# Fast-stage term loads moved to SyncE and shared between chunks, with a replanned instruction order

## The chip, the cores and the metric

The kernel runs as one program on one core of a Trainium2 chip. The metric is the device time of one execution in microseconds (us). The engines are TensorE (PE, matmuls; its weight loads are shown as PEld), VectorE (DVE), ScalarE (ACT), GpSimd (POOL) and SyncE (SP). Each engine takes its own instructions strictly in the order in which the program lists them; DMA transfers are issued from an engine's list too, and then run beside everything else.

## The reference

Two parts follow each other. The first is attention with a feature map, for 8 batches, 8 heads, 576 positions and 64 columns; the second takes its output as 4608 tokens of 512 numbers through a layer of 2048 hidden units with the Mish function.

```python
def phi(x):
    proj = np.einsum('bhsd,df->bhsf', x, w_phi)
    proj = proj - np.max(np.abs(proj), axis=-1, keepdims=True)
    return np.concatenate([np.exp(proj), np.exp(-proj)], axis=-1)
q_p, k_p = (phi(q), phi(k))
kv = np.einsum('bhsf,bhsd->bhfd', k_p, v)
z = np.sum(k_p, axis=2)
num = np.einsum('bhsf,bhfd->bhsd', q_p, kv)
den = np.einsum('bhsf,bhf->bhs', q_p, z)[..., None] + 1e-06
x = num / den                       # seen as [4608, 512]
...
h = x @ w_in                        # [4608, 2048]
sp = np.where(h > 20.0, h, np.log1p(np.exp(np.minimum(h, 20.0))))
return ((h * np.tanh(sp)) @ w_out)  # [4608, 512]
```

## The kernel before

**Tiling.** The tokens are cut into 18 chunks `c` of 256. A chunk needs two attention units, `q{c}_0` and `q{c}_1` (two pairs of heads each), and the sums over keys that they read, which come from 36 key units `k{n}`. For a chunk the hidden layer has 16 tiles `f` of 128 units: `ff_in` (L508) makes one tile with 12 matmuls of 128x256 on PE ("h" in the profile). Numbers are split into a high and a low part, so each product takes three matmuls.

**Output product, plain and fast.** Chunks 0 to 4 multiply by `w_out` directly (`ff_out`, L542, "o" in the profile). From chunk `FAST` = 5 on, two hidden tiles 2m and 2m+1 make a pair of tiles `m` (0 to 7), and `out_fast` (L668) multiplies a pair with 21 matmuls of 128x256 by a scheme with seven products instead of eight ("ox", "oy", "oz", "ow"). Its second operands are sums and differences of blocks of `w_out`. They are computed once (`w_sum`, `combine`; planned from `PREP` with a step of `PSTEP`), sent to DRAM as `terms[m]`, five per pair, and loaded back into SBUF when they are needed: `load_term(c, m, i)` (L661) moves term `i`, 256 KB. The fifth term of every pair stays in SBUF after chunk 5. The other four go into a ring of eight slots, so the terms of pair m can be loaded once the fast product of pair m-2 has been made, and they are loaded again in every chunk. The last two pairs of the last chunk use four tiles of their own ("late").

**A unit's path.** For a query unit: `project` (PE, L327, "pp_q"), maximum and subtraction (DVE, L331 and L339, "m_q" and "e_q"), a block transpose of each of its two halves (DVE, L351), then each half goes to DRAM (`q_send`, SP, L355, "there_e<-e_q") and comes back with four DMAs that finish the transpose (`q_fetch`, SP, L360, "e_q<-there_e"). ACT takes the two exponentials of each half (L428, L429), PE makes the sums over keys ("kvps") and the numerators ("num", both L347), DVE adds and copies the key sums (L411, L414) and divides (L466 to L468). The result goes through DRAM in the same way ("there_x<-via", then "x<-there_x") to become the operand xTh, xTl of `ff_in`. The next unit is projected right after the numerators, when DVE has given a PSUM bank back. `mish_fast` (ACT, L584), `mix` (DVE, L592 to L594), `mix_cast` (ACT, L599) and `mix_rest` (DVE, L603) make the operands of `out_fast`. The exponential and Mish need different tables in ACT; ACT_TABLE_LOAD changes them.

**What sets the order.** No engine chooses anything at run time. The class `Plan` holds a task for each of these steps, with an engine, a key (roughly its due time in tiles of `ff_in`), an assumed duration, its inputs, and the buffers ("rings") that it takes and gives back. `Plan.order()` plays the program through with those assumed durations. An engine that is free takes the first ready task by key, and the sequence so found is the order that is written into the engines' lists. Some tables of numbers (`FIRST_KEYS`, `WKEYS` and so on) are such keys. On the chip a task waits for its real inputs, and everything behind it on that engine waits too. In the kernel before, `order()` gives transfers of POOL and transfers of SP each a bandwidth of their own. Term loads are issued by POOL, and all other transfers by SP.

Of the kernel before, what the change touches and what calls it, by code (L numbers as in the profile page):

```python
# [31 lines left out]
FAST = 5  # L32
NLATE = 2
PAIRED = 0
PSTEP = 2.0
# [3 lines left out]
PREP = 54.0  # L39
# [9 lines left out]
FIRST_KEYS = {0: -16.15, 1: -12.2, 2: -13.99, 3: -10.24, 4: -8.03, 5: 7.54, 6: 8.15, 7: 8.48, 8: 11.95, 9: 27.01, 10: 29.1}  # L49
FIRST_QUERIES = {0: -11.57, 1: -9.11, 2: -2.36, 3: -2.32, 4: 13.79, 5: 9.72}  # L50
NFIRST = 6
E0 = -0.153
E1 = 0.109
GX = 0.616
ET = 0.242
WKEYS = [-9.37, -8.76, -5.05, -1.08, 3.01, 4.23, 4.64, 9.45, 6.86, 10.03, 12.05, 14.27, 15.1, 15.51, 17.23, 20.83,
         22.94, 21.2, 23.28, 26.21, 25.97, 28.3, 28.45, 32.87, 35.29, 34.63, 36.82, 37.72, 39.36, 40.32, 39.03, 41.85]
LAG, TAIL, TAILLAG = 4, 10, 2
TWOH = 99
NEAR = 1.4  # L60
LANDS = 2.297
BEHIND = 1.286
TEXP = 1.065
TLEAD = 2.999
SPLITC = 12
QFIRST = 99
URGENT = 2.075
UCENTRE = -0.038
BURST = ("sum", "num", "project")
PATIENCE = 1.514  # L70


class Plan:
# [11 lines left out]
    def order(self):  # L85
# [6 lines left out]
        now, table, bus, last = 0.0, None, [2.5, 2.5], dict(kind=None)  # L92
# [11 lines left out]
        def ready(task):  # L104
            if any(dep not in done for dep in task["after"]):
                return False
            for dep in task["deps"]:
                if done.get(dep, 1e9) > now:
                    return False
            if any(done.get(dep, 1e9) > now + NEAR for dep in task["near"]):  # L110
                return False
            for ring, _ in task["take"]:
                held_now = sum(released.get(token, 1e9) > now for token in slots.setdefault(ring, []))
                if held_now + sum(r == ring for r, _ in task["take"]) > self.rings.get(ring, 1):
                    return False
            return True

        while any(waiting.values()):
            moved = False
            for engine, queue in waiting.items():  # L120
# [45 lines left out]
            if not moved:  # L166
                times = [t for t in list(free.values()) + list(done.values()) if t > now + 1e-9]
# [7 lines left out]
def attention_then_mish(ctx, tc, qT, kT, va, w_phi, w_in, w_out, out):  # L175
# [10 lines left out]
    plan = Plan(dict(att=4, h=2, o=2, raw=NRAW, e=NE, v=NV, kv=NKV, half=NHALF, xT=NXT, g=NG, u=NU, w=NW, part=NPART, mix=NMIX, fast=2))  # L186
# [461 lines left out]

    def home_of(c, m, i):
        if c == NCH - 1 and m >= NFT // 2 - NLATE and i < 4:  # L650
            tile_of, k = divmod(4 * (m - NFT // 2 + NLATE) + i, 2)
# [5 lines left out]
        else:  # L657
            r = (4 * ((c - FAST) * NFT // 2 + m) + i) % (NFT // 2)
        return half_of(r, 1 - r % 2)

    def load_term(c, m, i):  # L661
        nc.gpsimd.dma_start(home_of(c, m, i).bitcast(F32), terms[m][:, i])  # L662

    def out_fast(c, m):
        if m == 0:
# [15 lines left out]
        for k, half, (ah, al), (bh, bl) in products:  # L681
            for n, (a, b) in enumerate(((ah, bh), (ah, bl), (al, bh))):
                nc.tensor.matmul(ps[k][:, half], a, b, start=(m == n == half == 0), stop=(m == NFT // 2 - 1 and n == 2),  # L683
# [190 lines left out]
    loaded = []  # L874

    def plan_fast(n, c, m):
# [10 lines left out]
        uses = []  # L887
        for i in range(5):
            q = 4 * ((c - FAST) * NFT // 2 + m) + i if i < 4 else f"{m} kept"
            if i == 4 and c > FAST:  # L890
                continue
            again = i < 4 and q >= NFT // 2
            r = q % (NFT // 2) if i < 4 else NFT // 2 + m
            deps = [] if again else [plain_out(FAST - 1, r)] + [f"wsum {r // 2} {r % 2}"]
            take, after = [(f"hs{r}", f"hs:{q}")], [loaded[q - NFT // 2]] if again else []
            if c == NCH - 1 and m >= NFT // 2 - NLATE and i < 4:
                nth = 4 * (m - NFT // 2 + NLATE) + i
                q = f"late {nth}"
                take, after = [] if nth % 2 else [("e", f"late:{nth // 2}")], [f"term {c} {m} {i - 1}"] if nth % 2 else []
# [47 lines left out]
    for n in range(total):  # L947
# [3 lines left out]
            take=[] if f % 2 else [("h", f"h:{c}_{f // 2}")], give=[f"xT:q{c}_{g}" for g in range(2)] if f == NFT - 1 else [])  # L951
# [72 lines left out]
```

## Time and profile before

| | |
|---|---|
| median of 3 runs | 1112.04 us (1109.36 to 1113.77) |
| the profiled execution, its own time | 1114.26 us |
| its span, first to last instruction | 1112.5 us |
| mean granted TensorE clock | 0.989 |
| DVE, ACT, POOL busy in the span | 729.4 us, 678.1 us, 227.2 us |
| term loads (POOL) | 424 of 256 KB |
| all DMA | 241.96 MB, 217 GB/s on average |

A row of a group view names the source line, the engine, the operation, and its output and inputs by the program's names ("h<-xTh,win"), with shape and count; then busy time, mean nanoseconds of one, and the idle time of the engine just before such instructions, with what ended it. A row of the timeline begins with its start in us from the span's start and its length; an idle time before it and what ended it stand in square brackets. "SPq" and "POOLq" rows are the issuing of DMAs.

### The profile page before, as it was taken

The numbers are of one execution on the slowest core, as the hardware profiler recorded it, in microseconds if no ns is written. First come the engines' busy times: TensorE is split into PE (matmuls) and PEld (weight loads), VectorE is DVE, ScalarE is ACT, GpSimd is POOL, SyncE is SP. The second block draws the span as 40 slices with busy tenths as digits, with TensorE's granted clock in tenths as the row PEclk, the third lists the DMA queues.
The fourth block names the chain that finished last, engine by engine and source line by source line (L and its number), as shares of the span: only waits on it lengthen the run. The fifth ranks groups of instructions, "written<-read, shape, count | busy, mean of one in ns | idle before, by whom it ended". The sixth has DMA issues, their size and how long they took to land.

```text
span 1112.5 us, 29851 instructions
## 1 busy us (share of the span) xinstructions
PE 1053.4 (95%) x12208; PEld 1001.7 (90%) x12208; DVE 729.4 (66%) x1668; ACT 678.1 (61%) x1019; POOL 227.2 (20%) x430
## 2 busy tenths in 40 slices
PE   7899999999999999999999999999999998989996
PEld 6888989999988989989889899999999988989996
DVE  6999995687855657666565557666767665656442
ACT  5688895566656555557666676776666645344431
POOL 0000000000011222223223232333232322332441
PEclk9999999999999999999999999999999998999998
DMA  9588643365674676757676778778677757777673
GB/s 353 189 267 291 229 134 101 120 208 179 208 228 146 203 228 214 242 180 246 208 235 212 232 235 255 240 232 264 209 256 233 230 181 241 220 229 228 233 231 130
DMA packets 138953, 241.96 MB, mean 217 GB/s; under 512 B 17984, under 2 KB 74432, under 8 KB 138816
## 3 DMA queue, kind: packets, MB, share of 16 engines
q1 hardware_dynamic: 104896, 128.87, 36.3%
q0 software_dynamic: 33920, 111.18, 31.2%
q8 instruction: 96, 1.57, 0.6%
q14 instruction: 41, 0.34, 0.1%
HBM read 196.46 MB, written 43.52 MB: 216 GB/s over the span
## 4 chain that ended last, share of the span: by engine, by line
PE 56%; DMA 17%; ACT 11%; DVE 9%; issue 3%; SPq 2%; POOL 0%; ACTq 0%; DVEq 0%
PE h L518 20%; PE o L553 9%; DMA e_q<-there_e 5%; PE num L347 5%; PE kvps L347 5%; DMA there_e<-e_q 4%; PE ox L683 4%; DMA x<-there_x 3%; PE oy L683 3%; PE ow L683 3%; PE pp_q L327 2%; PE pp_k L327 2%; SPq L360 2%; PE oz L683 2%; DMA raw_q<-qT 2%
## 5 line engine op out<-in xcount | busy, mean ns | idle before, releaser
L518 PE MATMUL h<-xTh,win 128*128 128x256 f32 x2304 | 439.9, 283 | 3.5 <-ACT u L584 1.9
L662 POOL DMA_DIRECT2D wout<-terms x416 | 222.2, 538 | 865.3 <-PE ow L683 504.9
L518 PEld LDWEIGHTS h<-xTh,win 128*128 128x128 f32 x2304 | 366.0, 189 | 10.2 <-ACT u L584 2.9
L518 PE MATMUL h<-xTl,win 128*128 128x256 f32 x1152 | 324.2, 281 | 0.3 <-DVE xTl L502 0.3
L518 PEld LDWEIGHTS h<-xTl,win 128*128 128x128 f32 x1152 | 218.0, 189 | 2.6 <-DVE xTl L502 0.5
L603 DVE TENSOR_TENSOR sl<-s,sh 128x640 fp32r<-128x640 f32 x104 | 85.6, 823 | 146.5 <-ACT sh L599 111.3
L599 ACT CAST sh<-s 128x640 fp32r<-128x640 f32 x104 | 74.8, 720 | 123.4 <-DVE s L594 107.5
L584 ACT ACTIVATE u<-h 128x512 f32<-128x512 f32 x104 | 62.2, 598 | 91.6 <-PE h L518 90.9
L553 PE MATMUL o<-wout,gh 128*128 128x512 f32 x320 | 101.8, 399 | 0.0
L347 PE MATMUL num<-kv,e_q 128*64 128x66 f32 x2304 | 79.3, 225 | 18.5 <-issue 8.6
L592 DVE TENSOR_TENSOR s<-u 128x256 f32<-128x256 f32 x104 | 42.7, 411 | 81.1 <-ACT u L584 80.9
L347 PEld LDWEIGHTS num<-kv,e_q 128*64 128x64 f32 x2304 | 73.3, 139 | 23.7 <-issue 9.7
L683 PE MATMUL ox<-wout,gh 128*128 128x256 f32 x408 | 82.3, 294 | 8.4 <-DMA wout<-terms 8.3
L347 PEld LDWEIGHTS kvps<-v,e_k 128*64 128x64 f32 x2560 | 78.2, 137 | 10.6 <-issue 3.1
L347 PE MATMUL kvps<-v,e_k 128*64 128x66 f32 x2560 | 83.9, 223 | 3.6 <-ACT e_k L383 1.9
L683 PE MATMUL oy<-wout,sh 128*128 128x256 f32 x416 | 79.6, 284 | 0.0
L683 PE MATMUL ow<-wout,sh 128*128 128x256 f32 x408 | 77.2, 281 | 0.0
L683 PEld LDWEIGHTS ox<-wout,gh 128*128 128x128 f32 x408 | 63.6, 192 | 12.3 <-DMA wout<-terms 6.8
L428 ACT ACT_TABLE_LOAD x41 | 52.6, 1283 | 36.1 <-DMA e_q<-there_e 35.7
L584 ACT ACT_TABLE_LOAD x53 | 68.0, 1283 | 0.9
L553 PEld LDWEIGHTS o<-wout,gh 128*128 128x128 f32 x320 | 55.7, 188 | 10.2
L683 PEld LDWEIGHTS oy<-wout,sh 128*128 128x128 f32 x416 | 64.8, 191 | 0.0
(107 smaller groups left out, 1897.0 us busy)
## 6 DMA issues: line engine op xcount, KB each, us to landing
wout<-terms POOLq DMA_DIRECT2D x416, 256.0 KB, 4.5
there_e<-e_q SPq DMA_DIRECT2D x60, 256.0 KB, 4.0
e_q<-there_e SPq DMA_DIRECT2D x240, 64.0 KB, 4.2
v<-va SPq DMA_DIRECT2D x32, 330.0 KB, 5.0
raw_k<-kT SPq DMA_DIRECT2D x36, 256.0 KB, 4.0
out<-osb SPq DMA_DIRECT2D x36, 256.0 KB, 3.3
raw_q<-qT SPq DMA_DIRECT2D x33, 256.0 KB, 4.3
words_in<-w_in SPq DMA_DIRECT2D x16, 512.0 KB, 6.1
```

Source lines behind the costliest of these rows:

```text
L327: nc.tensor.matmul(ps[j][:, n], raw[rows, n * P:(n + 1) * P], w_phi2[rows], start=True, stop=True)
L347: nc.tensor.matmul(ps[rows], lhsT[h], rhs[h], start=start, stop=stop, skip_group_check=True)
L360: nc.sync.dma_start(dst[32 * b:32 * b + 32].rearrange("i (a m) -> i a m", a=4), src[:, b * P:(b + 1) * P].rearrange("(a i) m -> i a m", a=4))
L428: nc.scalar.activation(e[:, 1, :], e[:, 0, :], AF.Exp)
L518: nc.tensor.matmul(ps, w[:, wcol], x[:, cc % 2, :], start=(n == 0), stop=(n == 11))
L553: nc.tensor.matmul(ps.rearrange("p (k n) -> p k n", k=2), g[:, cols], w, start=(i == first and k == 0), stop=(i == end and k == 2))
L584: nc.scalar.activation(u, h_live.pop((c, fp)).rearrange("p f s -> p (f s)"), AF.Mish)
L592: nc.vector.tensor_tensor(s[:, :CH], u[:, :CH], u[:, CH:], op=ALU.add)
L599: nc.scalar.copy(mix_high[c, fp], mixed[c, fp])
L603: nc.vector.tensor_sub(mix_low[c, fp], mixed.pop((c, fp)), mix_high[c, fp].bitcast(F32))
L662: nc.gpsimd.dma_start(home_of(c, m, i).bitcast(F32), terms[m][:, i])
L683: nc.tensor.matmul(ps[k][:, half], a, b, start=(m == n == half == 0), stop=(m == NFT // 2 - 1 and n == 2), skip_group_check=True)
```

## The change

**Reversed order.** In chunks 6, 8, ... 16 the pairs of tiles are taken from m = 7 down to m = 0, both in `ff_in` and in `out_fast`. `place_of(c, m)` is the place of a pair in its chunk. A chunk therefore begins with the two pairs with which the chunk before it ended, and their eight ring slots still hold the right terms: loads for places 0 and 1 are dropped in chunks 6 to 17. This leaves 424 - 96 = 328 term loads. `start` and `stop` of the accumulation follow the place.

**SyncE.** `load_term` is issued with `nc.sync`, and its task belongs to SP with an assumed 0.42 us. In the plan each such load takes one of `NFLIGHT` = 4 places of a ring "flight", which it gives back when the plan thinks that it has landed. This limits the order only; on the chip nothing waits for it.

**Plan.** For PE tasks after 190 us of planned time, inputs and buffers count as ready up to `-SLACK` = 0.137 us ahead of the planned moment (the constant is negative). All transfers share one assumed bandwidth. Many keys and constants get new values.

```diff
-PSTEP = 2.0
+PSTEP = 1.508
+NFLIGHT = 4
+SLACK = -0.137
-PREP = 54.0
+PREP = 58.757
-FIRST_QUERIES = {0: -11.57, 1: -9.11, 2: -2.36, 3: -2.32, 4: 13.79, 5: 9.72}
+FIRST_QUERIES = {0: -10.8, 1: -8.56, 2: 1.41, 3: -2.12, 4: 12.8, 5: 11.39}
-LANDS = 2.297
+LANDS = 2.451
-TLEAD = 2.999
+TLEAD = 3.609
...
         def ready(task):
+            limit = now - SLACK * (task["engine"] == "PE" and now > 190)
             for dep in task["deps"]:
-                if done.get(dep, 1e9) > now:
+                if done.get(dep, 1e9) > limit:
                     return False
...
                 if found["size"]:
-                    n = engine == "POOL"
-                    bus[n] = max(bus[n], now + took + 0.6) + found["size"] / (250e3 if n else 330e3)
-                    late = max(bus[n] - now - took, LANDS) + BEHIND
+                    bus = max(bus, now + 1.0) + found["size"] / 350e3
+                    late = max(bus - now - took, LANDS) + BEHIND
...
+    def place_of(c, m):
+        return NFT // 2 - 1 - m if c >= FAST and (c - FAST) % 2 else m
...
-            r = (4 * ((c - FAST) * NFT // 2 + m) + i) % (NFT // 2)
+            r = 4 * (m % 2) + i
         return half_of(r, 1 - r % 2)

     def load_term(c, m, i):
-        nc.gpsimd.dma_start(home_of(c, m, i).bitcast(F32), terms[m][:, i])
+        nc.sync.dma_start(home_of(c, m, i).bitcast(F32), terms[m][:, i])
...
-                nc.tensor.matmul(ps[k][:, half], a, b, start=(m == n == half == 0), stop=(m == NFT // 2 - 1 and n == 2),
+                nc.tensor.matmul(ps[k][:, half], a, b, start=(first and n == half == 0), stop=(end and n == 2),
...
-    tiles += [(c, f) for c in range(3, NCH) for f in range(NFT)]
+    tiles += [(c, 2 * place_of(c, f // 2) + f % 2) for c in range(3, NCH) for f in range(NFT)]
...
+            if kind == "ring" and c > FAST and place < 2:
+                ends.append(loaded[m % 2, i][1])
+                continue
...
-            add(f"term {key} {i}", "POOL", n + 0.5 + LAGF - TLEAD + 0.1 * i, 1.2, lambda i=i: load_term(c, m, i),
-                deps=deps + [f"send {m} {min(i // 2, 2)} {p}" for p in range(2)], take=take, size=262144,
-                after=after)
+            add(f"term {key} {i}", "SP", n + 0.5 + LAGF - TLEAD + 0.1 * i, 0.42, lambda i=i: load_term(c, m, i),
+                deps=deps + [f"send {m} {min(i // 2, 2)} {p}" for p in range(2)], size=262144, after=after,
+                take=([] if kind == "late" and nth % 2 else [(slot, token)]) + [("flight", f"flight:{key} {i}")],
+                give=[f"flight:{key} {i}"])
```

Since the plan sets the order, the change moves instructions on every engine. Three places show what matters below. The lines of the changed kernel have numbers that are 2 to 7 higher: L355, L360 and L351 become L357, L362 and L353; the term load L662 becomes L668.

The first place is SP's list around unit q9_0 in the fast stage. "there_e_9_0" is the DRAM copy of one of its halves, "x_1" belongs to the unit before it. Before, the list reads:

```order
L355 DMA there_x_1_7207<-via_1_7182 128x512
L355 DMA there_e_9_0_7252<-e_q_0_7211 128x512
L360 DMA x_1_7163<-there_x_1_7207 32x4x128 x4
L360 DMA e_q_0_7211<-there_e_9_0_7252 32x4x128 x4
L355 DMA there_e_9_0_7334<-e_q_0_7213 128x512
L360 DMA e_q_0_7213<-there_e_9_0_7334 32x4x128 x4
```

The change has there:

```order
L357 DMA there_x_1_7178<-via_1_7153 128x512
L668 DMA wout_0_826<-terms_3930 128x512
L668 DMA wout_0_882<-terms_3930 128x512
L668 DMA wout_0_1059<-terms_3930 128x512
L668 DMA wout_0_1145<-terms_3930 128x512
L357 DMA there_e_9_0_7222<-e_q_0_7182 128x512
L362 DMA x_1_7134<-there_x_1_7178 32x4x128 x4
L357 DMA there_e_9_0_7270<-e_q_0_7184 128x512
L362 DMA e_q_0_7182<-there_e_9_0_7222 32x4x128 x4
L668 DMA wout_0_1395<-terms_4151 128x512
L362 DMA e_q_0_7184<-there_e_9_0_7270 32x4x128 x4
```

Four term loads stand ahead of the unit's first send and one between its two fetches; the second half is now sent before the first half is fetched, and no longer after it. Before, the second send stands behind the first fetch in 12 of the 24 units q6_0 to q17_1; in the change it stands ahead of the first fetch in all 24.

The second place is DVE's list at the same unit: the two transposes of its halves (STREAM_TRANSPOSE), and between them work for pair 5 and for a key unit ("m_k", "e_k"). Before:

```order
L351 STREAM_TRANSPOSE e_q_0_7211<-e_q_0_7211 128x512
L608 TENSOR_TENSOR gl_5_7246<-u_5_7098,gh_5_7100 128x256
L603 TENSOR_TENSOR sl_5_7254<-s_5_7228,sh_5_7244 128x640
L331 TENSOR_REDUCE m_k_7282<-pp_k_7234 128x4
L331 TENSOR_REDUCE m_k_7285<-pp_k_7235 128x4
L339 TENSOR_TENSOR e_k_7287<-pp_k_7234,m_k_7282 128x512
L339 TENSOR_TENSOR e_k_7302<-pp_k_7235,m_k_7285 128x512
L351 STREAM_TRANSPOSE e_q_0_7213<-e_q_0_7213 128x512
```

The change:

```order
L353 STREAM_TRANSPOSE e_q_0_7182<-e_q_0_7182 128x512
L610 TENSOR_TENSOR gl_5_7220<-u_5_7062,gh_5_7064 128x256
L605 TENSOR_TENSOR sl_5_7236<-s_5_7200,sh_5_7218 128x640
L353 STREAM_TRANSPOSE e_q_0_7184<-e_q_0_7184 128x512
L333 TENSOR_REDUCE m_k_7264<-pp_k_7206 128x4
```

The key unit's four instructions have moved behind the second transpose.

The third place is the end of PE's list, in the last chunk. Rows "ox" are the beginnings of fast products and rows "ow" their ends; the number behind "gh_" or "sh_" is the pair. Before, the product of pair 4 follows that of pair 3 directly, as that one follows pair 2 and all later ones follow each other:

```order
L683 MATMUL ow_14926<-wout_0_1419,sh_3_14960 128x256 x2
L683 MATMUL ow_14926<-wout_0_1419,sl_3_14976 128x256
L683 MATMUL ox_14923<-wout_0_1144,gh_4_14955 128x256 x2
L683 MATMUL ox_14923<-wout_0_1144,gl_4_15022 128x256
L683 MATMUL ox_14923<-wout_0_983,gh_4_14955 128x256 x2
```

In the change, the rows ahead of pair 4 are matmuls of `ff_in`:

```order
L520 MATMUL h_14_14995<-xTh_1_14505,win_3_2155 128x256
L520 MATMUL h_14_14995<-xTh_1_14505,win_3_2281 128x256
L520 MATMUL h_14_14995<-xTl_1_14529,win_3_2281 128x256
L520 MATMUL h_14_14995<-xTh_1_14505,win_3_2281 128x256
L690 MATMUL ox_14803<-wout_0_1145,gh_4_14856 128x256 x2
```

There, one tile of h (12 matmuls) stands between pairs 2 and 3, two tiles between pairs 3 and 4, and none behind pair 4. In the first fast chunk the change puts two tiles of h between the products of pairs 4 and 5, where before none stood. Between the projection of a unit q{c}_0 and its numerators, PE's list for most of the chunks 7 to 16 had 7 tiles of h and 4 fast products before, and has 8 and 5 in the change; for q{c}_1 it had 9 and 4 (or 3), and has 8 and 3.

On ACT the exponentials of a unit's two halves were in most units parted by a Mish; in the change they stand side by side, and the list has 130 ACT_TABLE_LOAD where it had 158.

More of the change, by code (lines that the diff above doesn't have):

```diff
@@ L91, in order @@
         done, slots, released, freed = {}, {}, {}, {}
-        now, table, bus, last = 0.0, None, [2.5, 2.5], dict(kind=None)
+        now, table, bus, last = 0.0, None, 2.5, dict(kind=None)
         issued = []
@@ L112, in ready @@
             for ring, _ in task["take"]:
-                held_now = sum(released.get(token, 1e9) > now for token in slots.setdefault(ring, []))
+                held_now = sum(released.get(token, 1e9) > limit for token in slots.setdefault(ring, []))
                 if held_now + sum(r == ring for r, _ in task["take"]) > self.rings.get(ring, 1):
@@ L185, in attention_then_mish @@
     banks = dict(att=ps_att, h=ps_h, o=ps_o)
[L186 removed]
+    plan = Plan(dict(att=4, h=2, o=2, raw=NRAW, e=NE, v=NV, kv=NKV, half=NHALF, xT=NXT, g=NG, u=NU, w=NW, part=NPART, mix=NMIX, fast=2, flight=NFLIGHT))
     nc.scalar.preload_act_table_set("natural_log_exp_and_others")
@@ L886, in plan_fast @@
             give=[f"s:{key}"])
-        uses = []
+        uses, place = [], place_of(c, m)
+        late, ends = place - NFT // 2 + NLATE, [f"g:{key}", f"mix:{key}", f"sh:{key}", f"sl:{key}"]
         for i in range(5):
-            q = 4 * ((c - FAST) * NFT // 2 + m) + i if i < 4 else f"{m} kept"
-            if i == 4 and c > FAST:
+            nth, kind = 4 * late + i, "kept" if i == 4 else "late" if c == NCH - 1 and late >= 0 else "ring"
+            if kind == "kept" and c > FAST:
                 continue
[L892 to L899, printed above, removed]
-            add(f"term {key} {i}", "POOL", n + 0.5 + LAGF - TLEAD + 0.1 * i, 1.2, lambda i=i: load_term(c, m, i),
-                deps=deps + [f"send {m} {min(i // 2, 2)} {p}" for p in range(2)], take=take, size=262144,
-                after=after)
-            if i < 4:
-                loaded.append(f"term {key} {i}")
-            uses.append((f"term {key} {i}", f"hs:{q}"))
@@ new lines, in plan_fast @@
+            if kind == "ring" and c > FAST and place < 2:
+                ends.append(loaded[m % 2, i][1])
+                continue
+            r = 4 * (m % 2) + i if i < 4 else NFT // 2 + m
+            slot, token, after = f"hs{r}", f"hs:{key} {i}", []
+            deps = [plain_out(FAST - 1, r), f"wsum {r // 2} {r % 2}"]
+            if kind == "ring":
+                if (m % 2, i) in loaded:
+                    deps, after = [], [loaded[m % 2, i][0]]
+                loaded[m % 2, i] = f"term {key} {i}", token
+                if c == NCH - 1 or place < NFT // 2 - 2:
+                    ends.append(token)
+            elif kind == "late":
+                slot, token, deps = "e", f"late:{nth // 2}", []
+                after = [f"term {key} {i - 1}"] if nth % 2 else []
@@ L908, in plan_fast @@
-        if c == FAST and m == 0:
+        take = [("o", f"ox:{c}"), ("o", f"oz:{c}"), ("fast", f"oy:{c}"), ("fast", f"ow:{c}")] if place == 0 else []
+        if c == FAST and place == 0:
             take += [("att", "reserved 0"), ("att", "reserved 1")]
-        add(f"out {key}", "PE", when, 2.48, lambda: out_fast(c, m), deps=[f"low {key}", f"mixl {key}"] + [d for d, _ in uses], after=[before_out],
-            take=take, give=[f"g:{key}", f"mix:{key}", f"sh:{key}", f"sl:{key}"] + [t for _, t in uses if t[-4:] != "kept"])
+        add(f"out {key}", "PE", when, 2.48, lambda: out_fast(c, m), deps=[f"low {key}", f"mixl {key}"] + uses, after=[before_out],
+            take=take, give=ends)
```

47 lines of the change are left out of this document (24 added, 23 removed).

## The prediction

> **What bounds the kernel now.** First I read the busy shares on the page, then the busy time by stage.
>
> ```profile
> PE 1053.4 (95%) x12208; PEld 1001.7 (90%) x12208; DVE 729.4 (66%) x1668; ACT 678.1 (61%) x1019; POOL 227.2 (20%) x430
> 0.00:190.00 190.00, 175.27 (x2216) 157.19 (x2218) 163.09 (x366) 147.56 (x234) 0.70 (x6) 1.00 0.66 227
> 190.00:400.00 210.00, 207.54 (x2369) 191.28 (x2365) 143.76 (x312) 126.78 (x204) 17.29 (x32) 1.00 0.58 182
> 400.00:1076.00 676.00, 643.09 (x7417) 626.15 (x7417) 410.90 (x962) 396.67 (x570) 200.68 (x376) 0.99 0.73 229
> 1076.00:1112.50 36.50, 27.48 (x217) 27.07 (x215) 11.69 (x29) 7.14 (x13) 8.54 (x16) 0.91 0.46 155
> ```
>
> A stage row holds its length, then the busy time of PE, PEld, DVE, ACT and POOL, the granted clock, the DMA share and GB/s. PE is the bound, and the change takes no matmul away. What it can win is PE's idle time and slow clock: 14.7 us idle up to 190 us, 2.5 us up to 400, 32.9 us up to 1076 and 9.0 us in the last 36.5 us. The groups of PE's instructions from 400 us on say before what it idles:
>
> ```profile
> L518 PE MATMUL h<-xTh,win 128*128 128x256 f32 x1544 | 293.6, 283 | 3.5 <-ACT u L584 1.9 <-ACT xTh L496 1.6
> L683 PE MATMUL ox<-wout,gh 128*128 128x256 f32 x392 | 79.3, 294 | 8.4 <-DMA wout<-terms 8.3
> L347 PE MATMUL num<-kv,e_q 128*64 128x66 f32 x1408 | 49.2, 227 | 15.1 <-issue 7.4 <-ACT e_q L429 3.4 <-DVE kv L411 3.2
> L327 PE MATMUL pp_q<-w_phi,raw_q 64*128 64x128 f32 x336 | 28.5, 291 | 9.4 <-DVE r L466 3.6 <-DMA raw_q<-qT 3.0 <-DVE x L468 2.8
> ```
>
> The numerators and the projection behind them idle 15.1 + 9.4 = 24.5 us, and the fast products wait 8.4 us for terms. To see why the numerators are late I followed one unit, q9_0, in the timelines of SP, DVE, ACT and PE.
>
> ```profile
> 513.21 1.28 PE L327 MATMUL pp_q<-w_phi,raw_q 64*128 64x128 f32 x16
> 518.79 0.33 SPq L355 DMA_DIRECT2D there_e<-e_q  x1
> 519.22 1.93 SPq L360 DMA_DIRECT2D x<-there_x  x4
> ...
> 519.74 1.29 DVE L331 TENSOR_REDUCE m_k<-pp_k 128x4 f32<-128x512 f32 x2
> 522.14 0.70 DVE L351 STREAM_TRANSPOSE e_q<-e_q 128x512 f32<-128x512 f32 x1
> 523.03 1.73 SPq L360 DMA_DIRECT2D e_q<-there_e  x4
> 524.86 0.37 SPq L355 DMA_DIRECT2D there_e<-e_q  x1
> 531.15 1.76 SPq L360 DMA_DIRECT2D e_q<-there_e  x4
> ...
> 535.82 2.56 PE L347 MATMUL kvps<-v,e_k 128*64 128x66 f32 x80
> 536.29 1.28 ACT L428 ACT_TABLE_LOAD   x1 [0.20 <-DMA e_q<-there_e]
> 538.78 0.71 ACT L599 CAST sh<-s 128x640 fp32r<-128x640 f32 x1
> 540.61 0.42 DVE L414 COPY kv<-kvps 128x264 f32<-128x264 f32 x1
> 540.79 0.42 PE L347 MATMUL num<-kv,e_q 128*64 128x66 f32 x7 [2.41 <-issue]
> ```
>
> Projection ends at 514.5. The first half is sent at 518.8, the second only at 524.9: its transpose stood behind the key unit on DVE, and its send behind the first fetch, which sat in SP's list until 523.0. So the second fetch is issued at 531.15 and landed at 536.3, when ACT's wait ends. Then come table, exponentials, the cast, DVE's L603 and the key sums that stand behind it: 4.5 us from landing to numerators (536.3 to 540.8). PE had nothing to do from 538.4 on. "issue" hides that chain: DVE's copy ends as PE starts.
>
> **The change part by part.**
>
> *Both halves sent before the first fetch.* In the new order the second transpose follows at once on L603, so it could start near 519.7 instead of 522.1. The four term loads ahead of the first send cost SP time that was POOL's:
>
> ```profile
> q1 hardware_dynamic: 104896, 128.87, 36.3%
> q0 software_dynamic: 33920, 111.18, 31.2%
> 517.61 2.13 POOL L662 DMA_DIRECT2D wout<-terms  x4 [10.28 <-PE ow L683]
> ```
>
> POOL needed 2.13 us for four; an SP issue of a send or fetch above takes 0.33 to 0.48 us, so I take 0.43 us for an SP term load, the trace having none (ends 0.33 and 0.53), or 1.7 us for four. Starting at 517.6, they end at 519.3, the first send moves from 518.8 to 519.3, the x fetch ends at 521.3, and the second send goes at 521.4, 3.5 us earlier than before. At the same distances (6.3 us from send to fetch, 5.1 to landing) the second half lands at 532.8.
>
> PE meanwhile has more to do ahead of these numerators: one more tile of h and one more fast product.
>
> ```profile
> 223.38 1.42 PE h L518 x12
> 1086.59 0.40 PE L683 MATMUL ox<-wout,gh 128*128 128x256 f32 x2
> 1089.07 0.40 PE L683 MATMUL ox<-wout,gh 128*128 128x256 f32 x2
> 1089.64 2.14 POOL L662 DMA_DIRECT2D wout<-terms  x4 [4.63 <-PE ow L683]
> 1095.58 0.79 PE L683 MATMUL ox<-wout,gh 128*128 128x256 f32 x2 [3.83 <-DMA wout<-terms]
> ```
>
> A tile takes 1.42 us, a fast product 1089.07 - 1086.59 = 2.48 us, together 3.9 us. The key sums would end near 542.3, while landing plus 4.5 us is 537.3. So a wait of 2.4 us turns into 5.0 us to spare. Units q{c}_1 lose about as much: they have 8 tiles and 3 products instead of 9 and 4. But beside them the change loads no terms for two places. What that is worth shows in the stretch 200:300, where no terms are loaded (first row), against 400:1112 (the other two):
>
> ```profile
> e_q<-there_e SPq DMA_DIRECT2D x32, 64.0 KB, 2.0
> wout<-terms POOLq DMA_DIRECT2D x384, 256.0 KB, 4.6
> e_q<-there_e SPq DMA_DIRECT2D x176, 64.0 KB, 4.8
> ```
>
> A fetch lands in 2.0 us there and in 4.8 us beside terms. A unit without terms beside it gets back up to 2.8 us on a fetch and about as much on a send, more than the 3.9 us. A later unit of before, q11_1, has both sends together, with the terms still there:
>
> ```profile
> 666.29 1.16 PE L327 MATMUL pp_q<-w_phi,raw_q 64*128 64x128 f32 x16
> 671.94 0.91 SPq L355 DMA_DIRECT2D there_e<-e_q  x2
> 677.26 5.64 SPq L360 DMA_DIRECT2D e_q<-there_e  x8
> ```
>
> Its last fetch is issued 15.5 us after its projection (667.45 to 682.9) against 18.4 us for q9_0 (514.5 to 532.9), and its numerators start without a wait. Projections that wait for DVE's L466 and L468 are the same lateness one step on. Bounds: between 0 and -24.5 us. I take three quarters, **-18.5 us**, as the 3.0 us for raw_q and the tight units need not go.
>
> *Terms and the end.* The last three rows above show pair 4 of the last chunk. Pair 2's product ends as pair 3's begins, at 1089.07; then pair 4's terms are issued, and they have landed at 1095.58, 6.5 us later, with only one product of 2.48 us between. In the change two tiles of h follow pair 3, so between the end of pair 2 and pair 4 stand 3 x 1.42 + 2.48 = 6.7 us, no wait. For pair 5 it is 2 x 1.42 + 2.48 = 5.3 us, 1.2 us short. In chunk 5 two tiles come between pairs 4 and 5, 2.8 us against the 2.59 us that PE idled there (row below). Of 8.4 us I keep 1.4: **-7 us** (bounds 0 and -8.4). Dropping 96 loads, 25 of 242 MB, is counted at nothing beyond this; PE's matmuls hide it, and without that cover it would show in these same waits.
>
> *Clock.* There are five stretches at half clock; the wait ahead of the first, then the first and the last:
>
> ```profile
> 406.50 0.77 PE L683 MATMUL ox<-wout,gh 128*128 128x256 f32 x2 [2.59 <-DMA wout<-terms]
> 406.10:409.50 3.40, 3.00 (x14) 3.04 (x15) 1.76 (x3) 2.67 (x4) 0.44 (x1) 0.50 1.05 300
> 1095.60:1099.00 3.40, 3.40 (x16) 3.40 (x17) 0.00 (x0) 0.00 (x0) 0.00 (x0) 0.50 0.57 214
> ```
>
> The others are of 3.4, 6.8 and 3.4 us, 20.4 us in all, each behind a wait of 2 to 4 us. At half clock they cost at most half of that, 10.2 us. If three quarters of the waits go, **-7 us** (bounds 0 and -10.2).
>
> The Trainium skill, "TensorE: Matmul & The Clock Gate", section "Part 1: The HAM clock gate (the "warmup" mystery)", gives an idle window of about 3.4 us as what throttles. By that rule only the wait of 3.83 us would count and the clock term would be about -1.7 us, the sum 1089 us. The trace disagrees: the half clock of the first stretch came with a wait of 2.59 us.
>
> *Costs.* 328 issues of 0.43 us on SP are 141 us in a list that is mostly waiting; what counts is who stands behind them. The x fetch, the second half's send and the loads of raw_q do. The 1.6 us that h waits for xTh (in the first group row) show that x can be late, so I add **+2 us** (0 to 20, were that wait to come in each of 12 chunks). The 0.137 us by which PE may be planned early is a wait of at most that in a burst: 24 units make 3 us at the most; taken as nothing, since the lead of 5 us covers it. The start has new keys, but the same work on the same engines, with DVE 163 of 190 us busy: **0** (within 5 us either way, a third of the 14.7 us idle there).
>
> Sum: -18.5 - 7 - 7 + 2 = -30.5 us. From the profiled execution's own 1114.3 us (span 1112.5) this gives 1083.8, **1084 us**. That execution lies 2.2 us above the median of 1112.0, inside the spread of the three runs (1109 to 1114), so I leave that in.
>
> **The rivals.**
>
> *Slower: SP becomes the queue that PE waits for.* Term loads wait in SP's list for a fast product, and every send and fetch behind them waits too; their bytes go ahead of the fetches in one queue. Four loads are 1.05 MB; by the q0 row 111.18 MB took 31.2% of 1112.5 us, 320 GB/s, so 3.3 us. For: landing went from 2.0 to 4.8 us when terms ran. Against: 5.0 us to spare. With eight loads ahead (6.5 us) and one group held (1.7 us) a unit q{c}_0 is late by 8.2 - 5.0 = 3.2 us, 13 units make 42 us in place of the 24.5, and the clock stays: 1114 + 17 - 7 = 1124 us. It decides from about 7.4 us of extra delay on, where 13 x 2.4 us equals 24.5 + 7.
>
> The Trainium skill, "DMA: Bandwidth & Descriptors", section "Queues, rings and completion order", says that a DMA engine takes turns packet by packet between queues, while descriptors of one queue are taken in ring order. By that a fetch would now stand behind whole term loads. The trace cannot show it, since no terms ran on SP's queue.
>
> *Half a gain: the units q{c}_1 now wait.* They have 8 tiles and 3 products. If their landings improve by nothing, they lose 3.9 us of time ahead of the numerators; with an estimated 2.4 us to spare before, 12 units wait 1.5 us, +18 us: 1102 us.
>
> *No gain.* The plan ran on assumed durations, and its limit of four loads binds nothing on the chip. If the true lateness sits in the ACT and DVE lists and only changes its place, what is left is the 7 us at the terms, plus the 2 us on SP: 1109 us.
>
> *All of it goes*, start included: 1114 - 24.5 - 8.4 - 10 - 4 = 1067 us.
>
> **How the numbers follow.** Forecast (1072 to 1097) 0.62; half a gain 0.15; all of it 0.06; no gain 0.07; slower 0.10. The range 1066 to 1106 takes in the first three, 0.83. The measurement tells about 0.5% from no change, that is 1106.5 to 1117.6 us. Faster by more: 0.83; within: 0.07; slower: 0.10.
>
> **What would show it.** In the profile after, both sends of a unit stand next to each other or parted by the x fetch alone; the second fetch lands within 19 us of the projection; "num" and "pp_q" idle under 8 us in the fast stage and "ox" under 3 us; at most two stretches of half clock are left. The SP rival would show as waits of L357 and L362 behind term loads and later landings; half a gain as "num" waits in q{c}_1 alone. A start (up to 190 us) that is off by over 5 us would make the sum wrong without touching these steps.

## The result, and the profile after

| | kernel before | changed kernel |
|---|---|---|
| median of 4 runs each, same chip | 1111.41 us (1109.36 to 1113.77) | 1081.82 us (1078.59 to 1082.76) |
| ratio, 95% interval | | 0.9728 [0.9699, 0.9757] |
| the profiled execution, its own time | 1114.26 us | 1082.59 us |
| its span | 1112.5 us | 1080.8 us |

The change is faster by 2.7%; the forecast was 1084 us. The profiled spans differ by 31.7 us, against a sum of 30.5 us. Times are medians of all executions, while a ratio is to the kernel before as run beside it and leaves out executions in a slower state, so kernels of different rows are compared below by their ratios. The page's first row and the busy times by stage of the changed kernel (columns as before):

```profile
PE 1045.8 (97%) x12208; PEld 994.0 (92%) x12208; DVE 731.2 (68%) x1668; ACT 640.5 (59%) x991; POOL 0.7 (0%) x6
0.00:190.00 190.00, 177.87 (x2318) 158.65 (x2320) 164.65 (x371) 152.74 (x238) 0.70 (x6) 1.00 0.66 229
190.00:400.00 210.00, 209.56 (x2298) 193.22 (x2297) 145.55 (x311) 130.66 (x209) 0.00 (x0) 1.00 0.58 186
400.00:1076.00 676.00, 658.41 (x7599) 642.11 (x7597) 419.72 (x983) 357.14 (x545) 0.00 (x0) 0.99 0.62 198
1076.00:1080.80 4.80, 0.00 (x0) 0.00 (x0) 1.33 (x5) 0.00 (x0) 0.00 (x0) 0.99 0.29 109
```

With the same 12208 matmuls PE is busy 7.6 us less (1053.4 to 1045.8; half clock fell from 20.4 us to 6.8 us, which explains at most half of the difference, 6.8 us) and idles 24.1 us less (1112.5 - 1053.4 = 59.1, now 1080.8 - 1045.8 = 35.0). Where the idle time went is in the groups of PE's instructions from 400 us on:

```profile
L520 PE MATMUL h<-xTh,win 128*128 128x256 f32 x1536 | 289.8, 282 | 0.0
...
L690 PE MATMUL ox<-wout,gh 128*128 128x256 f32 x388 | 76.7, 290 | 16.8 <-DMA wout<-terms 16.7
...
L349 PE MATMUL num<-kv,e_q 128*64 128x66 f32 x1408 | 46.7, 222 | 0.3 <-DVE kv L413 0.2
...
L329 PE MATMUL pp_q<-w_phi,raw_q 64*128 64x128 f32 x336 | 26.8, 284 | 0.1
```

Numerators and projections ("num", "pp_q") fell from 24.5 us to 0.4, and h, with its xTl matmuls, from 3.8 to 0. But the fast products ("ox") now wait **16.8 us** for terms, where they waited 8.4. The page's list of DMA issues (KB each, median us from issue to landing) has the second change: a fetch lands in 2.1 us where it took 4.2 over the whole of the kernel before.

```profile
wout<-terms SPq DMA_DIRECT2D x320, 256.0 KB, 4.3
there_e<-e_q SPq DMA_DIRECT2D x60, 256.0 KB, 3.0
e_q<-there_e SPq DMA_DIRECT2D x240, 64.0 KB, 2.1
```

Unit q9_0 once more, in the timelines of PE, SP and ACT:

```profile
503.96 1.16 PE L329 MATMUL pp_q<-w_phi,raw_q 64*128 64x128 f32 x16
...
512.89 0.34 SPq L357 DMA_DIRECT2D there_e<-e_q  x1
515.06 1.73 SPq L362 DMA_DIRECT2D e_q<-there_e  x4
516.90 0.38 SPq L668 DMA_DIRECT2D wout<-terms  x1
517.38 1.79 SPq L362 DMA_DIRECT2D e_q<-there_e  x4
...
523.42 0.63 ACT L431 ACTIVATE e_q<-e_q 128x512 f32<-128x512 f32 x1
534.50 1.70 PE L349 MATMUL num<-kv,e_q 128*64 128x66 f32 x52
```

The second half is sent 7.8 us after the projection's end (before: 10.4), its last exponential ends at 524.05, and the numerators start at 534.50: the unit has 10 us to spare.

The new waits show in the timelines of SP and PE around 460 us, in the first reversed chunk:

```profile
453.23 0.37 SPq L357 DMA_DIRECT2D there_e<-e_q  x1
456.80 1.98 SPq L362 DMA_DIRECT2D e_q<-there_e  x4
458.88 0.37 SPq L668 DMA_DIRECT2D wout<-terms  x1
459.36 1.79 SPq L362 DMA_DIRECT2D e_q<-there_e  x4
461.19 1.38 SPq L668 DMA_DIRECT2D wout<-terms  x3
455.17 0.29 PE L690 MATMUL ow<-wout,sl 128*128 128x256 f32 x1
466.18 0.51 PE L690 MATMUL ox<-wout,gh 128*128 128x256 f32 x2 [1.19 <-DMA wout<-terms]
```

The product that frees the slots ends at 455.46. The terms for the product two places on could go then, but one goes at 458.88 and three from 461.19 on: SP stood at the first fetch until its send had landed, and issued the fetches first. PE waits 1.19 us at the end of it. For each kernel below I summed the idle time ahead of the 104 fast products by their place in the chunk; in the changed kernel 15.8 of 16.7 us lie at places 5 and 6, over most of the chunks.

### The profile page after: what moved, and what is told of

Its sections match the earlier page's. It is cut to its first block, busy times and chain, and to the rows that moved or that the text cites. A ratio compares the mean times of both kernels' runs of the same rounds, so it can differ in the third digit from the quotient of the medians.

```text
span 1080.8 us, 29566 instructions
## 1 busy us (share of the span) xinstructions
PE 1045.8 (97%) x12208; PEld 994.0 (92%) x12208; DVE 731.2 (68%) x1668; ACT 640.5 (59%) x991; POOL 0.7 (0%) x6
## 4 chain that ended last, share of the span: by engine, by line
PE 67%; DMA 8%; SPq 4%; DVE 4%; ACT 2%; issue 1%; DVEq 0%
PE h L520 27%; DMA wout<-terms 7%; PE o L555 7%; PE ox L690 6%; PE ow L690 5%; PE oy L690 5%; PE num L349 5%; PE kvps L349 5%; PE pp_q L329 3%; PE oz L690 3%; SPq L668 2%; PE pp_k L329 2%; DMA there_e<-e_q 1%; SPq L362 1%; SPq L321 1%
## 5 line engine op out<-in xcount | busy, mean ns | idle before, releaser
L690 PE MATMUL ox<-wout,gh 128*128 128x256 f32 x408 | 80.7, 290 | 16.8 <-DMA wout<-terms 16.7
L690 PEld LDWEIGHTS ox<-wout,gh 128*128 128x128 f32 x408 | 62.3, 188 | 21.8 <-DMA wout<-terms 18.8
L349 PE MATMUL num<-kv,e_q 128*64 128x66 f32 x2304 | 77.0, 223 | 2.6 <-ACT e_q L435 1.2
L555 PE MATMUL o<-wout,gl 128*128 128x512 f32 x160 | 63.3, 396 | 0.0
L690 PEld LDWEIGHTS ow<-wout,sh 128*128 128x128 f32 x408 | 63.3, 191 | 0.0
L690 PE MATMUL oy<-wout,sl 128*128 128x256 f32 x208 | 58.8, 283 | 0.0
```

Of the source, the lines that this page charges most:

```text
L349: nc.tensor.matmul(ps[rows], lhsT[h], rhs[h], start=start, stop=stop, skip_group_check=True)
L555: nc.tensor.matmul(ps.rearrange("p (k n) -> p k n", k=2), g[:, cols], w, start=(i == first and k == 0), stop=(i == end and k == 2))
L690: nc.tensor.matmul(ps[k][:, half], a, b, start=(first and n == half == 0), stop=(end and n == 2), skip_group_check=True)
```

## The experiments

Added lines shift the line numbers: by 18 in the first experiment, by 12 where `moved` edits the changed kernel's list behind the planner, by 1 in two others. "Idle" is PE's idle time from 400 us on.

### One part of the change alone, on the kernel before

**The sends.** The second transpose goes ahead of the key unit on DVE, the second send ahead of the first fetch on SP:

```diff
+            key = [i for i in range(at(f"regroup {u} 0"), second) if order[i]["name"].startswith("max k")]
+            if key:
+                order.insert(key[0], order.pop(second))
+            fetch, sent = at(f"turn {u} 0"), at(f"send {u} 1")
+            if fetch < sent:
+                order.insert(sent, order.pop(fetch))
```

> The kernel before, with two moves in its order and nothing else: in each unit of the fast stage the second transpose stands ahead of the key unit on DVE, and the first fetch behind the second send on SP. Theory A (the second half was sent too late): num and pp_q together idle under 12 us from 400 us on, where they idled 24.5, and the time is 1092 to 1101 us. Theory B (the waits went because term loads are fewer and on another queue): num and pp_q still idle over 20 us, time 1107 to 1114 us.

Measured: 1116.83 us, ratio 1.0023 [0.9971, 1.0074]. The groups of PE:

```profile
L701 PE MATMUL ox<-wout,gh 128*128 128x256 f32 x392 | 78.3, 292 | 12.1 <-DMA wout<-terms 12.1
...
L365 PE MATMUL num<-kv,e_q 128*64 128x66 f32 x1408 | 48.0, 225 | 9.9 <-issue 5.2 <-ACT e_q L447 2.5 <-DVE kv L429 1.2
...
L345 PE MATMUL pp_q<-w_phi,raw_q 64*128 64x128 f32 x336 | 29.1, 295 | 6.2 <-DVE r L484 3.6 <-DVE x L486 2.7
```

The lateness falls by 8.4 us only (24.5 to 16.1), waits for terms take 3.7 us of it back, and the time does not move. That lies between the two expectations: on the old lists the order of the sends is a part of the lateness, and alone it buys nothing.

**The queue.** Same lists, the term loads on SP:

```diff
-        nc.gpsimd.dma_start(home_of(c, m, i).bitcast(F32), terms[m][:, i])
+        nc.sync.dma_start(home_of(c, m, i).bitcast(F32), terms[m][:, i])
```

> Kernel before, the same lists on PE, DVE and ACT, its 424 term loads issued by SP in the planned sequence in place of POOL. Theory S (a term load that waits for a fast product holds every send and fetch behind it): ox over 20 us, num + pp_q over 24.5 us, 1125 us or more. Rival Q (one queue is what made the fetches of the changed kernel land in 2.1 us; that is worth more than the waiting): fetches land in 3 us or less, num + pp_q under 15 us, 1092 to 1106 us.

Measured: 1092.07 us, ratio 0.9804 [0.9756, 0.9851]. Groups of PE, then the issues:

```profile
L683 PE MATMUL ox<-wout,gh 128*128 128x256 f32 x388 | 80.0, 299 | 20.0 <-DMA wout<-terms 20.0
...
L347 PE MATMUL num<-kv,e_q 128*64 128x66 f32 x1408 | 46.1, 222 | 0.9 <-issue 0.4 <-DVE kv L411 0.2
```

```profile
wout<-terms SPq DMA_DIRECT2D x416, 256.0 KB, 4.0
there_e<-e_q SPq DMA_DIRECT2D x60, 256.0 KB, 3.1
e_q<-there_e SPq DMA_DIRECT2D x240, 64.0 KB, 2.9
```

This was the surprise: the part that I had booked as a cost is a gain of 2% by itself. All three numbers of rival Q came; of theory S only "ox" did, at its limit of 20 us. Send plus fetch takes 3.1 + 2.9 = 6.0 us instead of 4.0 + 4.2 = 8.2. In q9_0, ACT's wait for the second half ends 19.9 us after the projection (before: 21.8), though the second send still stands behind the first fetch, and the numerators follow without a wait. A margin of some 2 us was missing in this unit, and this restores it. What it gives back is seen in the other row: "ox" 8.4 to 20.0 us.

**The bytes.** Lists and queue of before, the 96 loads left out:

```diff
-        nc.gpsimd.dma_start(home_of(c, m, i).bitcast(F32), terms[m][:, i])
+        if i == 4 or c == FAST or m > 1:
+            nc.gpsimd.dma_start(home_of(c, m, i).bitcast(F32), terms[m][:, i])
```

> Kernel before, its lists unchanged and terms on POOL, without the loads of pairs 0 and 1 in chunks 6 to 17 (96 loads left out; those products use what is in the slots). Theory D (the bytes beside the fetches are a part of the late numerators): fetches land at 3.5 us or less, num + pp_q 8 to 16 us (from 24.5), 1093 to 1104 us. Rival U (the order of sends alone makes them late, as the run with late sends on the changed kernel suggests): fetches over 4 us, num + pp_q over 20 us, 1105 to 1114 us.

Measured: 1101.07 us, ratio 0.9886 [0.9848, 0.9924]. In the issues, then in the groups of PE:

```profile
there_e<-e_q SPq DMA_DIRECT2D x60, 256.0 KB, 2.5
e_q<-there_e SPq DMA_DIRECT2D x240, 64.0 KB, 2.6
```

```profile
L347 PE MATMUL num<-kv,e_q 128*64 128x66 f32 x1408 | 49.1, 227 | 13.1 <-issue 7.7 <-ACT e_q L429 3.3 <-DVE kv L411 0.9
...
L327 PE MATMUL pp_q<-w_phi,raw_q 64*128 64x128 f32 x336 | 28.3, 296 | 0.8 <-DVE r L466 0.8
```

Theory D holds in its numbers: 25 MB less beside the fetches shorten the way there and back from 8.2 to 5.1 us in the median, and num + pp_q fall to 13.9 us, the time by 1.1%. But this is not the wait of q9_0. Of the 10.6 us, 8.6 are at "pp_q" and only 2.0 at "num". In the eight units q{c}_0 of chunks 8 to 15, of which q9_0 is one, the second half lands 21.6 us after the projection in the median (before: 21.7), and their numerators idle 12.5 us in all (before: 12.2).

### Undoing one part of the changed kernel

**Late sends**, in the 12 units in which before had them:

```diff
+        sent = at(f"send q{u} 1")
+        fetch = at(f"turn q{u} 0")
+        order.insert(fetch, order.pop(sent))
```

> The changed kernel; in the 12 units in which the kernel before had it so, the second send stands behind the first fetch on SP again. Nothing else moves. Theory A: the second fetch of q9_0 lands some 3 us later (18 to 20 us after the projection, not 15.8); units q{c}_0 hide it behind the extra tile and product, the four units q{c}_1 among the 12 wait up to 2 us each: 1082 to 1091 us, num and pp_q idle 1 to 9 us. Theory B: landings move by under 1 us and the time stays within 2 us of 1082.

Measured: 1102.0 us, ratio 0.9908 [0.9873, 0.9943], 20 us above the changed kernel. The group of "ox":

```profile
L702 PE MATMUL ox<-wout,gh 128*128 128x256 f32 x388 | 78.4, 294 | 28.5 <-DMA wout<-terms 28.5
```

The loss is large, but not where A put it: the numerators stay on time (num + pp_q 0.6 us). A late send holds SP, and it is the term loads behind it for which PE then waits. The rest is half clock: PE is busy 1055.2 us instead of 1045.8.

**All term loads on POOL**, the lists otherwise those of the changed kernel:

```diff
-        nc.sync.dma_start(home_of(c, m, i).bitcast(F32), terms[m][:, i])
+        nc.gpsimd.dma_start(home_of(c, m, i).bitcast(F32), terms[m][:, i])
```

> The changed kernel with the same order of tasks, but term loads issued by POOL from a list of their own. Theory C (the 16.8 us that ox now waits come from term loads standing behind sends and fetches in SP's list): ox idles under 6 us, fetches land later than 2.1 us but num and pp_q still idle under 6 us, 1066 to 1077 us. Theory D (terms are late because of bandwidth or because their slots come free late): ox idles 13 us or more; then fetches slow to over 4 us bring num waits back: 1080 to 1092 us.

Measured: **1072.43 us**, ratio 0.9647 [0.9585, 0.9710]:

```profile
L690 PE MATMUL ox<-wout,gh 128*128 128x256 f32 x388 | 76.5, 289 | 7.0 <-DMA wout<-terms 6.9
...
L349 PE MATMUL num<-kv,e_q 128*64 128x66 f32 x1408 | 47.5, 223 | 3.0 <-issue 1.6 <-DVE kv L413 1.0
```

Theory C holds, with "ox" a little above its figure. So SP, a gain on the old lists, is a loss on the new ones: it costs 9.8 us of "ox" and saves 2.7 us of "num". The two ratios differ by 0.8%, and their intervals overlap a little; the better version below leaves no overlap.

**Late halves with the terms on POOL**: as above, and in the 12 units the second transpose and send late. No term load stands behind these sends now.

```diff
+        late = [order.pop(at(f"{step} q{u} 1")) for step in ("regroup", "send")]
+        fetch = at(f"turn q{u} 0")
+        order[fetch:fetch + 1] = [late[0], order[fetch], late[1]]
```

> Changed kernel with the term loads on POOL, and in the 12 units in which the kernel before did so the second half's transpose is put late on DVE and its send behind the first fetch on SP. No term load is queued behind these sends now, so only the unit itself is late. Theory A of the prediction (the late second half makes the numerators wait): num + pp_q idle 12 to 25 us from 400 us on, 1083 to 1096 us. Rival P (PE's longer list between projection and numerators covers it; the late send hurts only what stands behind it on SP): num + pp_q under 6 us, 1070 to 1078 us.

Measured: 1101.14 us, ratio 0.9880 [0.9835, 0.9925]:

```profile
L361 PE MATMUL num<-kv,e_q 128*64 128x66 f32 x1408 | 54.6, 240 | 26.4 <-issue 15.7 <-DVE kv L425 5.6 <-ACT sh L613 2.5
```

Theory A's mechanism shows here, above its ranges: "num" goes from 3.0 to 26.4 us, while the fetches land in 2.4 us in the median, and the time rises by about 26 us by the two ratios (0.9880 against 0.9647). The longer list of PE between projection and numerators does not cover a late half. The size is not that of before, though: 26.0 of the 26.4 us are in the eight units q{c}_0 of chunks 8 to 15, where the second half now lands 23.2 us after the projection (before: 21.7) and the numerators follow 8.1 us later (before: 3.3; medians).

**The 96 loads put back**, first with the terms on SP, then on POOL:

```diff
+        if kind == "out" and rest[0].isdigit() and FAST <= int(rest[0]) < NCH - 1:
+            c, m = map(int, rest)
+            if plan.first_two(c + 1, m):
+                out += [dict(fn=lambda i=i, c=c, m=m: plan.load(c + 1, m, i)) for i in range(4)]
```

> The changed kernel with the 96 dropped loads put back: the terms of places 0 and 1 of chunks 6 to 17 are loaded again into the same slots, right after the product that read them last, from SP. Theory A (order, not bytes, made the gain): 41 us more of issuing on SP push ox waits up to 18 to 30 us, num and pp_q stay under 6 us: 1083 to 1094 us. Theory B (fewer bytes made the gain): num and pp_q idle over 15 us again, 1098 us or more.

> Changed kernel with the term loads issued by POOL and, in addition, the 96 shared loads put back (424 loads on POOL, none on SP; SP's list is that of the run that reached 1072.4 us). Theory S (with the terms off SP the sharing is worth little; the 38 us of the reload run were SP's list): 1070 to 1080 us, num + pp_q idle under 8 us from 400 us on, ox under 10 us. Rival D (the 25 MB themselves slow the fetches): fetches of a half land at 4.5 us or more, num + pp_q idle over 12 us, 1086 to 1100 us.

Measured: 1120.06 us on SP, ratio 1.0079 [1.0043, 1.0116]; 1096.17 us on POOL, ratio 0.9833 [0.9790, 0.9876]. The issues of the first and of the second:

```profile
wout<-terms SPq DMA_DIRECT2D x416, 256.0 KB, 4.4
there_e<-e_q SPq DMA_DIRECT2D x60, 256.0 KB, 4.8
e_q<-there_e SPq DMA_DIRECT2D x240, 64.0 KB, 2.0
```

```profile
wout<-terms POOLq DMA_DIRECT2D x416, 256.0 KB, 4.6
there_e<-e_q SPq DMA_DIRECT2D x60, 256.0 KB, 3.1
e_q<-there_e SPq DMA_DIRECT2D x240, 64.0 KB, 4.9
```

With these loads on SP the kernel is 0.8% slower than the kernel before. The time is on B's side of the first expectation, but num + pp_q, at 13.3 us, are over A's 6 us and under B's 15, and "ox", at 33.4 us, is over A's range; neither theory holds whole. On POOL the loads cost about 21 us by the two ratios (0.9833 against 0.9647), so theory S fails there. D is right in the time and in the fetches (4.9 us), but not in the place: num + pp_q are at 2.1 us, and it is "ox" that rises by 17.3 us, 15.7 us of it at place 0, whose loads had been dropped.

Place 0 also limits what the two runs say. In the reversed order it reads the terms of the same pair as place 7 just before it, so a load put back there starts only when that product is done. The runs price the loads in this order. A plan with the loads and without the reversal was not run.

### Parts of the planner

**Old numbers**: the tables and constants that both kernels have (`FIRST_KEYS` to `PATIENCE`, `PSTEP`, `PREP`) set back; `NFLIGHT` and `SLACK` kept.

> Changed kernel with the 17 tables and constants that both kernels have set to those of the kernel before (the new ones, NFLIGHT and SLACK, kept): reversal, sharing, SP and the planner's new rules alone. Theory N (the numbers only trim; the structure gives most of it): 1080 to 1093 us, num + pp_q under 8 us from 400 us on. Rival M (the re-tuned numbers made the order that fits): 1097 to 1112 us, num + pp_q over 12 us.

Measured: 1099.45 us, ratio 0.9884 [0.9822, 0.9946]. The time is M's, the numerators are N's: num + pp_q are at 1.2 us, "ox" at 21.2 us. The new numbers carry about 17 of the 30 us, and not through the numerators. In the profiled execution, 13.1 us longer than that of the changed kernel, 4.4 us are "ox", 3.0 us h, 1.2 us idle time before 400 us and 3.5 us a longer busy PE (1049.3 against 1045.8).

**No limit of four loads** (`NFLIGHT = 99`), and **no margin** (`SLACK = 0.0`):

> Changed kernel with the planner's limit of four term loads under way lifted (99); the order of some 70 rows of SP's list shifts, and little elsewhere. If the limit does nothing on the chip: 1078 to 1086 us, ox 14 to 20 us. Rival L (it keeps bursts of terms from standing ahead of sends and fetches): 1088 us or more, num + pp_q over 5 us or ox over 25 us.

> Changed kernel with the planner's margin SLACK set to 0, so that PE's list is planned without 0.137 us of early starts. If the margin is worth nothing measurable: 1078 to 1086 us. Rival V (it is what keeps PE's next work ahead of the units' arrivals): 1088 us or more, num + pp_q over 5 us.

Measured: 1082.67 us, ratio 0.9709 [0.9684, 0.9734], and 1083.34 us, ratio 0.9720 [0.9695, 0.9745]. Both are the changed kernel within its interval, and their "ox" (17.1 and 17.9 us) is close to its 16.8 us. These two parts are worth nothing that can be measured here.

### A better version

Terms for places 4 to 6 on POOL, the others on SP:

```diff
-        nc.sync.dma_start(home_of(c, m, i).bitcast(F32), terms[m][:, i])
+        queue = nc.gpsimd if place_of(c, m) in (4, 5, 6) else nc.sync
+        queue.dma_start(home_of(c, m, i).bitcast(F32), terms[m][:, i])
```

> Changed kernel, the term loads for places 4 to 6 of each chunk issued by POOL, the others by SP, in the planned order. Theory S (the 16.8 us of ox waits, 15.8 us of them at places 5 and 6, come from loads that stand in SP's list behind a unit's sends and fetches): ox under 9 us, num + pp_q under 4 us, 1069 to 1076 us, as with all loads on POOL. Rival W (those places wait because a load can only start when the product two places before is made, whichever queue issues it): ox 14 us or more, 1079 to 1085 us.

Measured: **1072.55 us**, ratio 0.9618 [0.9594, 0.9643]:

```profile
L691 PE MATMUL ox<-wout,gh 128*128 128x256 f32 x388 | 76.3, 289 | 7.7 <-DMA wout<-terms 7.7
...
L349 PE MATMUL num<-kv,e_q 128*64 128x66 f32 x1408 | 47.3, 223 | 2.7 <-issue 1.9 <-DVE kv L416 0.5
```

Theory S holds for the new lists. This version beats both kernels, by 3.8% and (from the two ratios) about 1.1%; with all terms on POOL it is as good.

### All runs side by side

Idle in us from 400 us on; send and fetch are the medians to landing; half clock is the number of stretches ahead of the last few us, where PE has ended.

| kernel | ratio | num + pp_q | ox | send, fetch | half clock |
|---|---|---|---|---|---|
| before | 1 | 24.5 | 8.4 | 4.0, 4.2 | 5 |
| before, early sends | 1.0023 | 16.1 | 12.1 | 3.8, 4.7 | 5 |
| before, terms on SP | 0.9804 | 1.5 | 20.0 | 3.1, 2.9 | 3 |
| before, 96 loads less | 0.9886 | 13.9 | 9.0 | 2.5, 2.6 | 4 |
| changed | 0.9728 | 0.4 | 16.8 | 3.0, 2.1 | 2 |
| changed, late sends | 0.9908 | 0.6 | 28.5 | 2.6, 2.0 | 7 |
| changed, loads put back | 1.0079 | 13.3 | 33.4 | 4.8, 2.0 | 9 |
| changed, old numbers | 0.9884 | 1.2 | 21.2 | 2.4, 2.0 | 5 |
| changed, no limit of four | 0.9709 | 0.4 | 17.1 | 3.2, 2.1 | 2 |
| changed, no margin | 0.9720 | 0.5 | 17.9 | 2.7, 2.1 | 0 |
| changed, POOL, loads put back | 0.9833 | 2.1 | 24.3 | 3.1, 4.9 | 4 |
| changed, POOL, late halves | 0.9880 | 26.7 | 3.7 | 3.4, 2.4 | 5 |
| changed, POOL | 0.9647 | 3.2 | 7.0 | 2.7, 2.7 | 1 |
| changed, POOL at places 4 to 6 | 0.9618 | 2.9 | 7.7 | 3.2, 2.4 | 0 |

## Why the prediction was right, and where it was not

The time came within 2.2 us, but four terms were off by more than that: the numerators by -5.6 us, the costs by -5.8, the start by -4.6 and the terms by +15.4. They nearly cancel, so that the closeness is luck; the direction is not.

**"Both halves sent before the first fetch", -18.5 us: -24.1 us.** The idle time of num + pp_q went to 0.4 us, the sends stand as forecast, and the second fetch of q9_0 is in at 15.8 us after the projection, under the 19 us named. In the eight units q{c}_0 of chunks 8 to 15 the second send goes 7.2 us after the projection instead of 11.1, the last of its four fetches lands 3.8 us after the issue of the first instead of 5.2, and the half is in at 16.1 us instead of 21.7 (medians). That a late half makes the numerators wait is shown by the late halves on POOL, which bring 23.5 us back. But the step kept the old landing of 5.1 us, and the shared queue is not in it. With the terms on POOL the landing in these units is 6.3 us, so the queue is what shortened it. On the old lists the sends bring 8.4 us, the bytes 10.6 us and the queue 23.0 us, each by itself: the sends and the queue make up for the same 2 us or so that units like q9_0 lacked, and the bytes act mostly at the projections. The three are therefore not to be added up. What PE's longer list and the exponentials side by side add to this was not tried apart.

**"Terms and the end", -7 us: +8.4 us. This is the step that failed,** and with it the sign "ox" under 3 us. Its places came out as worked out: pair 4 of the last chunk waits no longer, and pair 5 waits 1.1 us where 1.2 us were said. In chunk 5 the wait moved one pair on. What it left out are the chunks between: a term load that stands in SP's list behind a send and its fetch leaves some 6 us after its slot is free, as at 455.46 and 461.19, and the products at places 5 and 6 wait. With POOL for these loads "ox" falls to 7.7 us and the time by about 1%.

**"Clock", -7 us: -7.6 us** by PE's busy time, of which half clock can be 6.8 us; two stretches are left, behind waits of 2.73 and 2.01 us. The estimate of -1.7 us, by the 3.4 us of the Trainium skill, is too small; the last section shows what such a window does.

**"Costs", +2 us for x that is late: -3.8 us**, since h no longer idles at all. A load costs SP 0.46 us (1.38 us for three, row above), where 0.43 us was estimated. The price of SP came, but at the products, not at h.

**Start, 0:** -2.6 us of idle time up to 190 us and -2.0 us from there to 400, inside the 5 us either way.

The rival of SP as the queue that PE waits for was half right: it is one, for terms and not for units. Its argument that terms ahead of fetches make them land later fell with the runs on SP: fetches took 2.0 to 2.9 us there in the median. "Half a gain" fell with num at 0.3 us, "no gain" with the ratio. The 96 loads saved, counted at nothing "beyond this", are worth something: leaving them out gains 1.1% on the old lists, and putting them back into the new order costs about 21 us on POOL and 39 us on SP, by the ratios. What the sharing is worth against a plan made without it stays open.

Open remains how the 17 us of the new numbers split up. Each such run is one replanned order, and an order can be lucky.

## What to carry to other kernels

Where several short delays meet one deadline, each cure tried alone looks like the cause; put the suspected delay back into the fast version as well, as the late halves did, before naming one. A run that puts something back prices it in the order that was made without it, as the 96 loads at place 0 show. Moving a DMA to another engine's list does two things that can have opposite signs, the transfers that it shares a queue with and the waits that it stands behind, and the second depends on the order around it: SP gained 2% on one order and cost about 1% on the other. After a wait is gone, look at the group that grew, here "ox", since the next gain lies there.

## What the runs showed of the hardware

**A transfer on the queue of its neighbours.** With 424 term loads the fetches took 4.9 us when the terms ran on POOL's queue and 2.0 us when they shared SP's; the sends took 3.1 and 4.8 us. On one queue the send waits behind the terms, and when it has landed they mostly have too, so the fetch, which is issued only then, mostly finds no terms under way. The traces from 400 us on bear this out. On SP, 112 of the 169 fetches whose landing the trace gives were issued with no term load under way and landed in 2.0 us, the other 57 in 3.2 us; on POOL, 164 of 168 were issued beside a term load and landed in 5.3 us (medians).

The Trainium skill, "DMA: Bandwidth & Descriptors", section "Queues, rings and completion order", has turns between queues and ring order within one. That fits both rows; I had drawn only the delay of ring order from it, and overlooked that the dependent transfer behind it gains. The two queues also differ in kind: the page of the kernel before has POOL's as software_dynamic and SP's as hardware_dynamic. The move did not make the transfers themselves cheaper (all packets took 67.5% of 1112.5 us before, 67.8% of 1094.7 us with the old lists on SP), but no run put the terms on a second hardware queue, so the part of the kind is not separated.

**The clock looks at fixed windows.** In each of the 12 traces that have more than one, the half-clock stretches begin at multiples of 3.413 us from each other (before: 477.786 - 406.106 = 21 x 3.413). Windows on that grid in the changed kernel, in pairs of one with a wait and the next one:

```profile
814.46:817.87 3.41, 1.40 (x12) 1.20 (x12) 0.83 (x1) 3.36 (x5) 0.00 (x0) 1.00 0.99 332
817.87:821.29 3.42, 3.42 (x19) 3.42 (x18) 1.30 (x4) 1.11 (x3) 0.00 (x0) 0.50 0.43 165
759.80:763.21 3.41, 2.05 (x17) 1.84 (x16) 1.10 (x3) 1.63 (x3) 0.00 (x0) 1.00 0.82 247
763.21:766.62 3.41, 3.41 (x81) 3.27 (x81) 1.56 (x6) 0.72 (x1) 0.00 (x0) 1.00 0.20 76
```

2.01 us of idle PE in a window brought half clock in the next, 1.36 us did not. Over the 14 traces, of the windows at full clock after 100 us all 36 with 1.98 us or more idle were followed by half clock, 14 of the 27 with 1.64 to 1.97 us, and none of the 92 with 0.9 to 1.63 us. So a wait of 2.5 us can cost clock or not by how it falls on the grid. By these counts, a wait cut in two parts in different windows should save the clock though the idle time stays; no run tried that. The Trainium skill, "TensorE: Matmul & The Clock Gate", section "Part 1: The HAM clock gate (the "warmup" mystery)", describes such a free-running window of 3413 ns, and the grid agrees with it; that somewhat over half of one window idle suffices is what these rows add.
